# Issuing a kernel's loads in halves at four points of TensorE's progress

## The chip, the cores and the metric

The kernel runs on one core of one Trainium2 chip. The metric is device time in microseconds (us) of one execution; medians are of all runs of a job unless "fast" is said. A run is called slow when it is over 1.5% above the fastest run of its kernel. Ratios below are the mean time of one kernel's fast runs over that of the other's in the same rounds, so they are not quite the ratio of the medians quoted. In the views "PE" is TensorE and "PEld" its weight loads; "DVE", "ACT", "POOL" and "SP" are VectorE, ScalarE, GpSimd and SyncE, and a "q" behind a name is that engine's sequencer.

## The reference, cut to what matters

```python
B, Sq, D = 8, 112, 640
H, Sk, Dh = 32, 512, 192          # all inputs bf16
q = (x @ wq).reshape(B, Sq, H, Dh).transpose(0, 2, 1, 3)
p = softmax(einsum("bhqd,bhkd->bhqk", q, k_cache) * Dh ** -0.5)
o = einsum("bhqk,bhkd->bhqd", p, v_cache)
return o.transpose(0, 2, 1, 3).reshape(B, Sq, H * Dh) @ wo
```

K and V are 50 MB each and are read once, beside 7.9 MB each of wq and wo. So a load stream runs through the whole kernel.

## The kernel before

The work is cut into 64 units: eight head groups of four heads, times eight batches. In unit u TensorE does the scores S of unit u, PV of unit u-1, some tiles of the Q projection (Q) and of the output projection (O), the transposes T of unit u-1's output, and more Q or O tiles. The order is fixed. In the code, W(engine, semaphore, n) makes an engine wait until a semaphore has reached n; NU is the number of units, NK and NV the numbers of K and V buffers. In the views kr is a K buffer, kt its transpose, vs a V buffer, os the normalized output, and L840, L854, L863, L805 and L821 are the lines of S, PV, T, Q and O.

```python
for u in range(NU + 1):                 # TensorE
    if u < NU: do_S(u)                  # 96 matmuls, waits for K transposed by DVE
    if u > 0:  do_PV(u - 1)             # 16 matmuls, waits for V
    for it in items_at[u][0]: do(it)    # Q or O tiles
    if u > 0:  do_T(u - 1)              # waits for DVE's normalization of PV
    for it in items_at[u][1]: do(it)
```

DVE takes K's four transposes for unit u+2, the normalization NM of unit u-1 and the O evacuations strictly in this order. So a K that is late also holds up NM, and with it T on TensorE:

```python
for u in range(NU + 1):                 # DVE
    do_KT(u + 2, 0); do_KT(u + 2, 1)    # the first waits for K of u+2 and for S of u
    if u > 0: do_NM(u - 1)              # sums, 1/x, product into os_, which T reads
    do_KT(u + 2, 2) ...                 # cut: O evacuations, the last transpose
```

SP issues all loads. K and V have four buffers each. K needs a buffer whose transposes are done, V one whose PV is done:

```python
def load_k(u):
    if u >= NK: W(sp, vKT, 4 * (u - NK + 1))
    sp.dma_start(kr[u % NK]..., k_cache[...]).then_inc(mK[u % NK], 16)          # 768 KB
def load_v(u):
    if u >= NV: W(sp, pPV, u - NV + 1)
    for h in range(2):
        sp.dma_start(vs[u % NV][..., h, ...], v_cache[...]).then_inc(mV[u % NV], 16)  # 384 KB
...
for u in range(3, NU):
    load_k(u)
    load_v(u)
    if b == 3 and g + 2 < NG: load_wq(g + 2)    # 960 KB in one DMA
    if b == 6 and g + 1 < NG: load_wo(g + 1)    # 960 KB
```

V's wait is for the PV of four units back. When that ends, SP issues V(u), perhaps weights, and K(u+1) in a row: one burst per unit.

## Time and profile before

Median 472.49 us of 4 runs (468.73 to 478.7). The profiled run took 480.98 us and counts as slow (2.6% above the fastest).

The page of the kernel before; the digits are tenths of busy share, and of the granted TensorE clock, in 40 slices of the span.

```profile
span 479.1 us, 20206 instructions
PE 410.1 (86%) x8920; PEld 298.9 (62%) x8920; DVE 320.2 (67%) x634; ACT 220.9 (46%) x421; POOL 76.8 (16%) x280
PE   5859699999779999886999997779998878999893
PEclk9988899999979999998999999889998998999998
DMA  8997678989549798866689897576986864778711
q1 hardware_dynamic: 90256, 118.70, 74.7%
q8 instruction: 72, 1.18, 1.0%
PE 68%; DMA 10%; issue 10%; DVE 5%; SPq 5%; ACT 1%; DVEq 0%
```

TensorE is the busiest engine and most of the chain that ended last. It is idle for 479.1 - 410.1 = 69 us, the clock dips below full in some slices, and the DMA share swings from 4 to 9 tenths between neighbouring slices. The q8 line is easily passed over: 72 packets of 1.18 MB in all, 16 KB each, of kind "instruction". TensorE has 8920 matmuls and 8920 weight loads; 17840 / 72 = 248, so about one packet for every 250 of its instructions.

The view of waits of the kernel before (engine, line, what it waited for: us in total, times, longest):

```profile
PE ps L854 <- issue: 21.6, 8, 4.8
PE ps L840 <- issue: 14.1, 13, 3.3
PE ps L805 <- issue: 4.0, 3, 2.6
PE ps L863 <- DVE os L964: 7.6, 7, 3.3
DVE kt L952 <- DMA kr<-in_k_cache_dram: 20.5, 8, 4.3
```

"issue" means that the engine stood still and waited for nothing that the profile shows. With two lines of 2.8 us for L863 and L821, TensorE's waits of this kind add up to 45.3 us. L863 is T, which waits for DVE's NM: 7.6 us. What these waits are shows when the records of TensorE's instructions (matmuls, weight loads and those of its sequencer) are counted through in order: in the kernel before, in the changed kernel and in every run below, each "issue" wait of TensorE over 0.2 us after the first 10 us begins at the same place, 192 to 196 instructions past a multiple of 256. Below, the 256 instructions from one such place to the next are called a block, and the instruction packet that follows in order on a block's beginning (the one for the next block) a fetch.

One such wait in the timeline of the kernel before, TensorE's rows only (start, length, what, count, idle before and its releaser):

```profile
214.93 0.33 PE L854 MATMUL ps<-vs,pT 128*128 128x193 bf16 x2 [1.05 <-issue]
218.06 1.36 PE L840 MATMUL ps<-qT,kt 32*128 32x112 bf16 x96
219.35 0.59 PE L854 MATMUL ps<-vs,pT 128*128 128x193 bf16 x5
224.20 1.96 PE L854 MATMUL ps<-vs,pT 128*128 128x193 bf16 x11 [4.25 <-issue]
```

TensorE stops in the middle of PV, after 5 of 16 matmuls, where the program has no semaphore wait at all. The same stretch in 1 us windows (columns: window, its length, busy share of PE, PEld, DVE, ACT and POOL with instruction counts, then clock, DMA share, GB/s):

```profile
214.00:215.00 1.00, 0.07 (x1) 0.07 (x1) 0.35 (x1) 0.47 (x2) 0.00 (x0) 1.00 0.00 0
215.00:216.00 1.00, 1.00 (x7) 0.58 (x7) 0.63 (x4) 0.00 (x0) 0.17 (x1) 1.00 0.00 0
218.00:219.00 1.00, 1.00 (x77) 0.94 (x80) 0.96 (x2) 0.08 (x1) 0.00 (x0) 1.00 1.09 365
221.00:222.00 1.00, 0.00 (x0) 0.00 (x0) 0.16 (x1) 0.30 (x1) 0.00 (x0) 1.00 1.17 415
224.00:225.00 1.00, 0.80 (x6) 0.74 (x7) 0.00 (x0) 0.00 (x0) 0.00 (x0) 0.50 0.23 92
```

The loads go from nothing to 415 GB/s and back, and the clock drops to 0.50 at 223.1 us, while TensorE still stands, and stays there until 230.0. The trace's packet records add the last piece: the instruction packet that comes next in order here started at 221.86 us, 5.5 us into a burst whose packets began at 216.3, and TensorE resumed 1.4 us after it had landed.

### The profile page before, as it was taken

The page shows a single profiled execution, that of the slowest core. Times are in us where ns is not written, and L with a number is a line of the kernel's source. Part 1 is how long each engine was busy: PE and PEld are TensorE (multiplying, and loading weights), DVE is VectorE, ACT ScalarE, POOL GpSimd, SP SyncE. Part 2 cuts the span into 40 slices and gives each one's busy share as a digit, 9 for nine tenths or more (in the row PEclk, how much of TensorE's full clock was granted, in tenths as well). Part 3 has the DMA queues.
Part 4 walks back from the last instruction along what each step waited for, and adds up shares of the span by engine and source line. Part 5 has one row for each costly group of instructions (what it writes and reads, how often), then busy time and mean ns, then how long its engine had stood idle before and what let it go on. Part 6 is the DMA issues. An engine that isn't in the chain of part 4 may idle for free.

```text
span 479.1 us, 20206 instructions
## 1 busy us (share of the span) xinstructions
PE 410.1 (86%) x8920; PEld 298.9 (62%) x8920; DVE 320.2 (67%) x634; ACT 220.9 (46%) x421; POOL 76.8 (16%) x280
## 2 busy tenths in 40 slices
PE   5859699999779999886999997779998878999893
PEld 3436477766647777654777665547776555776672
DVE  2555478777657778755687778456785754788952
ACT  2535255455425555452455554336553553455440
POOL 1300122012110122101221122001230100111110
PEclk9988899999979999998999999889998998999998
DMA  8997678989549798866689897576986864778711
GB/s 311 360 367 247 216 267 264 311 251 341 191 137 332 257 313 289 297 216 218 234 277 299 270 319 233 166 234 217 342 276 206 275 235 148 263 232 297 233 44 34
DMA packets 90348, 120.04 MB, mean 251 GB/s; under 512 B 3472, under 2 KB 82064, under 8 KB 90256
## 3 DMA queue, kind: packets, MB, share of 16 engines
q1 hardware_dynamic: 90256, 118.70, 74.7%
q8 instruction: 72, 1.18, 1.0%
q14 instruction: 20, 0.16, 0.1%
HBM read 117.54 MB, written 1.15 MB: 248 GB/s over the span
## 4 chain that ended last, share of the span: by engine, by line
PE 68%; DMA 10%; issue 10%; DVE 5%; SPq 5%; ACT 1%; DVEq 0%
PE ps L821 17%; PE ps L854 16%; PE ps L840 15%; PE ps L805 14%; DMA kr<-in_k_cache_dram 10%; PE ps L863 5%; SPq L1088 3%; DVE kt L952 2%; DVE os L964 2%; SPq L1067 1%; SPq L1080 0%; PE ps L810 0%; ACT pT L910 0%; DVE rinv L960 0%; ACT oT L919 0%
## 5 line engine op out<-in xcount | busy, mean ns | idle before, releaser
L952 DVE STREAM_TRANSPOSE kt<-kr 128x384 int32<-128x384 int32 x256 | 208.5, 862 | 93.3 <-PE ps L840 72.8
L910 ACT ACTIVATE pT<-ps 128x448 bf16<-128x448 f32 x256 | 118.7, 548 | 92.3 <-PE ps L840 92.3
L854 PE MATMUL ps<-vs,pT 128*128 128x193 bf16 x1024 | 102.8, 254 | 22.7 <-issue 21.6
L821 PE MATMUL ps<-wos,oT 128*128 128x320 bf16 x672 | 113.3, 307 | 3.6 <-issue 2.8
L854 PEld LDWEIGHTS ps<-vs,pT 128*128 128x128 bf16 x1024 | 85.9, 100 | 30.5 <-issue 24.5
L840 PE MATMUL ps<-qT,kt 32*128 32x112 bf16 x6144 | 91.5, 210 | 14.8 <-issue 14.1
L840 PEld LDWEIGHTS ps<-qT,kt 32*128 32x128 bf16 x6144 | 79.0, 94 | 35.3 <-issue 31.7
L805 PE MATMUL ps<-xT,wqs 128*128 128x448 bf16 x420 | 96.2, 366 | 4.0 <-issue 4.0
L902 ACT ACTIVATE qT<-ps 128x448 bf16<-128x448 f32 x96 | 52.2, 545 | 92.1 <-PE ps L805 83.7
L821 PEld LDWEIGHTS ps<-wos,oT 128*128 128x128 bf16 x672 | 64.9, 101 | 34.4 <-issue 6.1
L919 ACT ACTIVATE oT<-ps 128x672 bf16<-128x672 bf16 x64 | 46.8, 731 | 59.3 <-PE ps L863 59.3
L1052 POOL TENSOR_SCALAR bad<-rinv 112x4 f32<-112x4 f32 x64 | 14.6, 228 | 363.6 <-DVE rinv L960 363.6
L964 DVE TENSOR_TENSOR os<-ps,rinv 112x768 bf16<-112x768 f32 x64 | 61.3, 958 | 2.5 <-DVE rinv L960 0.4
L805 PEld LDWEIGHTS ps<-xT,wqs 128*128 128x128 bf16 x420 | 40.8, 101 | 34.9 <-issue 9.8
L978 DVE TENSOR_TENSOR acc<-ps,acc 128x320 f32<-128x320 f32 x84 | 40.3, 480 | 11.3 <-PE ps L821 11.1
L863 PE MATMUL ps<-ident,os 112*128 112x112 bf16 x384 | 31.3, 219 | 10.5 <-DVE os L964 7.6
L863 PEld LDWEIGHTS ps<-ident,os 112*128 112x128 bf16 x384 | 22.1, 100 | 24.5 <-DVE os L964 21.5
L1041 POOL COPY wqs<-wqr 128x384 bf16<-128x384 bf16 x70 | 33.2, 507 | 18.4 <-DMA wqr<-in_wq_dram 16.5
L957 DVE TENSOR_REDUCE sm<-ps 112x4 f32<-112x8 f32 x64 | 10.2, 159 | 30.4 <-PE ps L854 30.3
L810 PE MATMUL ps<-xT,wqs 128*32 128x448 bf16 x240 | 14.9, 404 | 1.2 <-ACT xT L891 0.8
L1053 POOL TENSOR_SCALAR bad<-rinv 112x4 f32<-112x4 f32 x64 | 14.5, 226 | 4.0
L1055 POOL TENSOR_TENSOR cnt<-cnt,bad 112x8 f32<-112x8 f32 x64 | 12.9, 201 | 5.3
(30 smaller groups left out, 50.0 us busy)
## 6 DMA issues: line engine op xcount, KB each, us to landing
kr<-in_k_cache_dram SPq DMA_DIRECT2D x64, 768.0 KB, 7.1
vs<-in_v_cache_dram SPq DMA_DIRECT2D x128, 384.0 KB, 4.4
wos<-in_wo_dram SPq DMA_DIRECT2D x8, 960.0 KB, 8.6
wqr<-in_wq_dram SPq DMA_DIRECT2D x7, 960.0 KB, 8.3
out_dram<-xs SPq DMA_DIRECT2D x7, 160.0 KB, 2.7
wqs<-in_wq_dram SPq DMA_DIRECT2D x1, 960.0 KB, 6.4
xs<-in_x_dram SPq DMA_DIRECT2D x1, 640.0 KB, 4.3
xs<-in_x_dram SPq DMA_DIRECT2D x1, 480.0 KB, 8.5
```

The costliest lines, as they stand in the source:

```text
L805: mm = pe.matmul(ps[:, bank(it), 0:HQ], wqs[:, g % 2, dc, 128 * c:128 * (c + 1)], rhs, start=(dc == 0), stop=(dc == DC - 1))
L821: mm = pe.matmul(ps[:, bank(it), 0:HO], oT[:, c, 128 * m:128 * (m + 1)], wos[:, g % 2, c, HO * h:HO * (h + 1)], start=(c == 0), stop=(c == 5))
L840: mm = pe.matmul(ps[:, a, SQ * t:SQ * (t + 1)], kt[u % 2][p, t, c // 2, :, c % 2], qT[g % 2][p, c, SQ * b:SQ * (b + 1)], start=(c == 0), s ...
L854: mm = pe.matmul(pv[:, k, e, o0:o0 + DH + 1], pT[u % 2][:, a, t, :], vs[u % NV][:, a, t // 2, v0:v0 + DH + 1], start=(t == 0), stop=(t == ...
L863: mm = pe.transpose(psb[:, 4, o0:o0 + SQ], os_[u % 2][:, 128 * j:128 * (j + 1)], ident[0:SQ, 0:SQ])
L902: act.activation(qT[g % 2][:, c, HQ * h:HQ * (h + 1)], ps[:, bank(it), 0:HQ], ACTF.Copy).then_inc(aQ, 1)
L910: act.activation(pT[u % 2][:, a, :, 0:SQ], ps[:, a, 0:4 * SQ].rearrange("p (t q) -> p t q", t=4), ACTF.Exp, scale=scale).then_inc(aEX, 1)
L919: act.activation(oT[:, :, SQ * b:SQ * (b + 1)].rearrange("p (k c) q -> p k c q", k=2), src.rearrange("p k (c q) -> p k c q", c=3), ACTF.Co ...
L952: dve.transpose(dst, src).then_inc(vKT, 1)
L964: dve.tensor_tensor(os_[u % 2][:].rearrange("p (k e d) -> p k e d", k=2, e=2), pv[0:SQ, :, :, 1:1 + DH], rinv[:, u % 4, :].rearrange("p (k ...
L978: ins = dve.tensor_tensor(ob[:, m, cs] if g == NG - 1 else acc[:, m, cs], src, acc[:, m, cs], op=ALU.add)
L1041: ins = gp.tensor_copy(wqs[:, g % 2, dc, :].rearrange("p (k e a i) -> p e k a i", k=3, e=2, a=4)[:, e], wqr[:, dc, :].rearrange("p (a k i ...
```

## The change

The intent is an even load stream. K is halved as V already was; weights are cut into chunks of 160 and 192 KB. SP issues a piece after S, after PV, after the first items and after the second items of every unit, weights after PV. K is loaded three units ahead and V two. No compute instruction moves; outside SP only three wait counts change. The core of the diff (cuts marked):

```diff
-            for u in range(3, NU):
-                load_k(u)
-                load_v(u)
+            for u in range(NU):
+                W(sp, pS, 4 * (u + 1))
+                if u + 3 < NU:
+                    load_k(u + 3, 0)
+                W(sp, pPV, u)
+                if u + 3 < NU:
+                    load_k(u + 3, 1)
                 g, b = divmod(u, B)
-                if b == 3 and g + 2 < NG:
-                    load_wq(g + 2)
-                if b == 6 and g + 1 < NG:
-                    load_wo(g + 1)
+                if b < 3 and g + 2 < NG:
+                    for c in range(2 * b, min(2 * b + 2, DC)):
+                        load_wq(g + 2, c)
+                if b >= 3 and g + 1 < NG:
+                    load_wo(g + 1, b - 3)
+                # cut: the sixth wo chunk, and wo of group 0 in unit 0
+                if items_at[u][0]:
+                    after(items_at[u][0][-1])
+                if u + 2 < NU:
+                    load_v(u + 2, 0)
+                if items_at[u][1]:
+                    after(items_at[u][1][-1])
+                if u + 2 < NU:
+                    load_v(u + 2, 1)
```

At the start, K of unit 1 and V of unit 0 wait for one Q tile each, all of wq for group 1 follows, then K of unit 2 and V of unit 1 (not shown).

More of the change, by code (lines that the diff above doesn't have):

```diff
@@ L817, in do_O @@
                 if m == 0 and h == 0:
-                    W(pe, mWO[g % 2], 16 * (g // 2 + 1))
+                    W(pe, mWO[g % 2], 96 * (g // 2 + 1))
                 bank_free(pe, it)
@@ L947, in do_KT @@
                 if t == 0:
-                    W(dve, mK[u % NK], 16 * (u // NK + 1))
+                    W(dve, mK[u % NK], 32 * (u // NK + 1))
                     W(dve, pS, 4 * (u - 1))
@@ L1036, in reorder @@
                 if dc == 0:
-                    W(gp, mWQ[1], 16 * g)
+                    W(gp, mWQ[1], 16 * DC * g)
                     if g >= 2:
@@ L1063, in load_x, with load_wq0, load_wq, load_wo @@
                     "(m p) d -> p m d", p=128)).then_inc(mX[j], 16)
-            def load_wq(g):
+            def load_wq0():
+                sp.dma_start(wqs[:, 0], wq[:, 0:4 * DH].rearrange("(c p) n -> p c n", p=128)).then_inc(mWQ[0], 16)
+            def load_wq(g, c):
                 W(sp, gW, DC * (g - 1))
-                sp.dma_start(wqs[:, 0] if g == 0 else wqr[:], wq[:, 4 * DH * g:4 * DH * (g + 1)].rearrange(
-                    "(c p) n -> p c n", p=128)).then_inc(mWQ[min(g, 1)], 16)
-            def load_wo(g):
+                sp.dma_start(wqr[:, c, :], wq[128 * c:128 * (c + 1), 4 * DH * g:4 * DH * (g + 1)]).then_inc(mWQ[1], 16)
+            def load_wo(g, c):
                 if g >= 2:
                     W(sp, pO, 2 * MT * (g - 1))
-                sp.dma_start(wos[:, g % 2], wo[4 * DH * g:4 * DH * (g + 1)].rearrange("(c p) d -> p c d", p=128)
-                             ).then_inc(mWO[g % 2], 16)
-            def load_k(u):
+                r = 4 * DH * g + 128 * c
+                sp.dma_start(wos[:, g % 2, c, :], wo[r:r + 128]).then_inc(mWO[g % 2], 16)
+            def load_k(u, h):
                 g, b = divmod(u, B)
@@ L1079, in load_k, with load_v @@
                     W(sp, vKT, 4 * (u - NK + 1))
-                sp.dma_start(kr[u % NK][:].rearrange("p s d -> p (s d)"),
-                             k_cache[b, 4 * g:4 * g + 4].rearrange("a (j s) d -> (a j) (s d)", s=16)).then_inc(mK[u % NK], 16)
-            def load_v(u):
+                sp.dma_start(kr[u % NK][:, 8 * h:8 * h + 8].rearrange("p s d -> p (s d)"),
+                             k_cache[b, 4 * g:4 * g + 4].rearrange("a (j h s) d -> (a j) h (s d)", h=2, s=8)[:, h]
+                             ).then_inc(mK[u % NK], 16)
+            def load_v(u, h):
                 g, b = divmod(u, B)
@@ L1086, in load_v @@
                     W(sp, pPV, u - NV + 1)
-                for h in range(2):
-                    sp.dma_start(vs[u % NV][:, :, h, 32:32 + 2 * DH],
-                                 v_cache[b, 4 * g:4 * g + 4].rearrange("a (m h t) d -> h m a (t d)", h=2, t=2)[h]
-                                 ).then_inc(mV[u % NV], 16)
-            load_x(0)
-            load_wq(0)
-            load_k(0)
-            load_x(1)
-            load_k(1)
-            load_v(0)
-            load_wq(1)
-            load_v(1)
@@ L1100, in _ @@
-            load_k(2)
-            load_wo(0)
-            load_v(2)
-            for u in range(3, NU):
-                load_k(u)
-                load_v(u)
-                g, b = divmod(u, B)
-                if b == 3 and g + 2 < NG:
-                    load_wq(g + 2)
-                if b == 6 and g + 1 < NG:
-                    load_wo(g + 1)
+                sp.dma_start(vs[u % NV][:, :, h, 32:32 + 2 * DH],
+                             v_cache[b, 4 * g:4 * g + 4].rearrange("a (m h t) d -> h m a (t d)", h=2, t=2)[h]
+                             ).then_inc(mV[u % NV], 16)
@@ new lines, in after @@
+            def after(it):
+                if it[0] == "Q":
+                    W(sp, pQ, q_index[it[1:]] + 1)
+                else:
+                    W(sp, pO, o_index[it] + 1)
+            load_x(0)
+            load_wq0()
+            for h in range(2):
+                load_k(0, h)
+            load_x(1)
+            for n, fn, u in ((1, load_k, 1), (3, load_v, 0)):
+                for h in range(2):
+                    after(order[n - 1 + h])
+                    fn(u, h)
+            for c in range(DC):
+                load_wq(1, c)
@@ new lines, in _ @@
+            after(order[5])
+            for h in range(2):
+                load_k(2, h)
+            for h in range(2):
+                load_v(1, h)
+            for u in range(NU):
[5 more added lines that the diff above has]
+                    load_k(u + 3, 1)
+                g, b = divmod(u, B)
+                if b < 3 and g + 2 < NG:
[3 more added lines that the diff above has]
+                    load_wo(g + 1, b - 3)
+                if b == 0 and g >= 1:
+                    load_wo(g, 5)
+                if u == 0:
+                    for c in range(6):
+                        load_wo(0, c)
+                if items_at[u][0]:
[6 more added lines that the diff above has]
+                    load_v(u + 2, 1)
```

## The prediction

> **What bounds the kernel now.** TensorE. In the timeline an undisturbed unit takes 5.71 us from one score stage to the next (231.83 to 237.53), TensorE busy throughout. The shortest spacings of a head group's eight units add up to 47.7 us. Seven groups and the shorter last one would be 372 us; the trace has 442 us between first and last score stage. About 70 us is disturbance: 28 TensorE gaps over 0.7 us (52 us together), and windows at clock 0.5 after them (35 us of busy time at half speed).
>
> **What the gaps are.** Most are put down to "issue", nothing the profile shows (longest 4.8 us; 10% of the chain). They lie every 256 TensorE instructions and end 1.3 to 1.6 us after a 16 KB packet of queue 8 (about 1.0 us each) lands. [...] A fetch on quiet DMA (block begun at 140.33 us) starts 1.3 us later and is usable after 3.9 us; a block lasts 4.5 to 5.5 us, so that fits. A block begun at 214.93 was fetched at 221.86, near the end of a burst of V, wo and K, and TensorE stood 4.25 us. The kernel issues V, K and often 960 KB of weights together once per unit: 4 to 6.5 us of full DMA, then quiet (DMA share 1.0 and 0.0 in 1 us stretches). K landing late (DVE transposes wait 20.5 us in 8 waits) gives a few smaller gaps.
>
> **What the change does.** No compute instruction moves; only SP's list and three wait counts differ. 384 KB pieces go out after S, after PV, after the first items and at the unit's end, 1.3 to 1.7 us apart; each takes about 1.0 us at the bursts' 385 GB/s. Weights follow in chunks of 160 to 192 KB. The queue before a fetch shrinks from up to 6.5 us to 1 to 1.6 us. The long fetch stalls and most half-clock windows should go, leaving 10 us in short ones (estimate: a third of the blocks have only 0.6 to 0.8 us of slack).
>
> **What it costs.** More SP issues (0.5 us each, off the path). Prefetch is shorter: K's second half is issued 4.4 us before DVE needs it; a lone 384 KB piece took 3.3 us at best. DVE has almost no slack before T, so some lateness shows. The mean rate wanted rises to about 305 GB/s.
>
> **Sum.** 17 (first score stage) + 372 + 13 (tail) = 402; + 6 first group still loading much at once, + 10 residual fetch stalls, + 4 half clock and late K: **422 us**, range 402 to 450. Faster by over 2%: 0.93; within: 0.05; slower: 0.02.
>
> **What would show it.** Right: TensorE gaps over 2 us gone; "issue" under 20 us in the waits; spacing near 5.7 us in nearly all units; clock above 0.98; DMA share even at 0.75 to 0.9 over the slices. Wrong: "issue" gaps as long as before (bursts don't delay the fetch), or DVE waiting for K in most units.
>
> **What would make it wrong.** Pieces queue up anyway, since one unit's traffic is 80 to 85% of its time; K's latency above 4.4 us becomes the period; the fetch's delay is set by something other than queued bytes.

The 4.5 to 5.5 us for a block were the author's estimate, and so is the slack behind the 10 us; in the trace of the kernel before, the blocks last 4.7 to 10.1 us from start to start, stalls included, with a median of 6.1.

## The result

Median 445.27 us of 4 runs (442.45 to 449.84) against 472.49 us; ratio of the fast runs 0.9429, 95% interval 0.9336 to 0.9523. The repeat on another chip (e5 below) gave 0.945. The changed kernel is 5.7% faster, where the prediction had 422 us, about 10.6%.

The page of the changed kernel (a fast run), the same lines:

```profile
span 444.3 us, 20578 instructions
PE 399.6 (90%) x8920; PEld 293.0 (66%) x8920; DVE 317.5 (71%) x634; ACT 220.8 (50%) x421; POOL 76.8 (17%) x280
PE   4956999989979999998999899879999999998992
PEclk9998799999998999999999999989999999999998
DMA  7879799998887989998799899878889988999731
q1 hardware_dynamic: 100560, 118.71, 84.3%
q8 instruction: 71, 1.16, 1.1%
PE 68%; DMA 16%; DVE 6%; issue 5%; SPq 2%; POOL 1%; ACT 0%; DVEq 0%; POOLq 0%
```

The DMA slices are even now. TensorE's idle time is 444.3 - 399.6 = 44.7 us, 24.3 less than before, and its busy time is 10.5 us less although it executes the same instructions. That second part is nearly all the clock: nine windows at 0.5 before (35 us of busy time in them), four after (15.5 us), and half of the difference is 9.7 us. 24.3 + 10.5 is the whole 34.8 us between the two profiles. (The medians differ by 27 us, because the profile before was a slow run.)

The waits of the changed kernel:

```profile
PE ps L854 <- issue: 5.0, 4, 2.1
PE ps L840 <- issue: 4.6, 3, 2.8
PE ps L805 <- issue: 0.8, 1, 0.8
PE ps L863 <- DVE os L964: 17.7, 17, 4.6
DVE kt L952 <- DMA kr<-in_k_cache_dram: 38.3, 21, 7.5
```

TensorE's issue waits fell from 45.3 to 10.6 us. But DVE's waits for K nearly doubled, and T's waits for DVE rose from 7.6 to 17.7 us: +10.1 us against -34.7 us, a net of -24.6 us, which matches the idle time. The gain has a price, which one wait of T behind a late K shows in the timeline of the changed kernel (DVE's rows, then TensorE's):

```profile
389.31 1.57 DVE L952 STREAM_TRANSPOSE kt<-kr 128x384 int32<-128x384 int32 x2 [1.44 <-DMA kr<-in_k_cache_dram]
391.22 0.96 DVE L964 TENSOR_TENSOR os<-ps,rinv 112x768 bf16<-112x768 f32 x1
...
390.53 0.98 PE L821 MATMUL ps<-wos,oT 128*128 128x320 bf16 x6
392.23 0.47 PE L863 MATMUL ps<-ident,os 112*128 112x112 bf16 x6 [0.73 <-DVE os L964]
```

K came 1.44 us late for the transposes; the normalization behind them ended late, and TensorE stood 0.73 us before T.

The trace's records allow one more measure. For every block of 256 TensorE instructions, take the time from the block's first instruction to the start of the instruction packet that follows in order (the packet for the next block), leaving out the first eight blocks and the last:

```
kernel                        median us   longest us
before                        3.14        7.53
changed                       2.08        5.66
no K or V traffic (e3)        0.79        3.89
```

Where TensorE waited for a packet, it resumed 1.2 to 1.7 us after that packet had landed, in every one of these kernels. So the stall is set by when the packet starts, and that depends on the load traffic. Single values vary: a repeat of the changed kernel (e5) has 2.21 and 6.28 us.

### The profile page after: what moved, and what is told of

Its sections match the earlier page's. It is cut to its first block, busy times and chain, and to the rows that moved or that the text cites. A ratio compares the mean times of both kernels' runs of the same rounds, so it can differ in the third digit from the quotient of the medians.

```text
span 444.3 us, 20578 instructions
## 1 busy us (share of the span) xinstructions
PE 399.6 (90%) x8920; PEld 293.0 (66%) x8920; DVE 317.5 (71%) x634; ACT 220.8 (50%) x421; POOL 76.8 (17%) x280
## 3 DMA queue, kind: packets, MB, share of 16 engines
q1 hardware_dynamic: 100560, 118.71, 84.3%
## 4 chain that ended last, share of the span: by engine, by line
PE 68%; DMA 16%; DVE 6%; issue 5%; SPq 2%; POOL 1%; ACT 0%; DVEq 0%; POOLq 0%
PE ps L854 17%; PE ps L821 16%; PE ps L840 15%; DMA kr<-in_k_cache_dram 14%; PE ps L805 13%; PE ps L863 5%; DVE os L964 3%; DVE kt L952 3%; PE ps L810 1%; DMA wqr<-in_wq_dram 1%; POOL wqs L1041 1%; DMA xs<-in_x_dram 1%; SPq L1070 1%; SPq L1076 1%; PE ps L785 1%
## 5 line engine op out<-in xcount | busy, mean ns | idle before, releaser
L821 PE MATMUL ps<-wos,oT 128*128 128x320 bf16 x672 | 109.6, 300 | 1.1 <-ACT oT L919 0.8
L854 PE MATMUL ps<-vs,pT 128*128 128x193 bf16 x1024 | 99.4, 249 | 6.1 <-issue 5.0
L840 PEld LDWEIGHTS ps<-qT,kt 32*128 32x128 bf16 x6144 | 78.5, 94 | 24.3 <-issue 20.2
L805 PE MATMUL ps<-xT,wqs 128*128 128x448 bf16 x420 | 93.5, 359 | 0.9 <-issue 0.8
L840 PE MATMUL ps<-qT,kt 32*128 32x112 bf16 x6144 | 89.1, 210 | 5.3 <-issue 4.6
L854 PEld LDWEIGHTS ps<-vs,pT 128*128 128x128 bf16 x1024 | 83.9, 98 | 12.9 <-issue 7.1
L821 PEld LDWEIGHTS ps<-wos,oT 128*128 128x128 bf16 x672 | 63.1, 98 | 29.0 <-issue 1.4
L964 DVE TENSOR_TENSOR os<-ps,rinv 112x768 bf16<-112x768 f32 x64 | 61.3, 958 | 2.5 <-DVE rinv L960 0.4
L863 PE MATMUL ps<-ident,os 112*128 112x112 bf16 x384 | 30.4, 216 | 17.9 <-DVE os L964 17.7
L863 PEld LDWEIGHTS ps<-ident,os 112*128 112x128 bf16 x384 | 21.0, 99 | 34.9 <-DVE os L964 34.0
L1041 POOL COPY wqs<-wqr 128x384 bf16<-128x384 bf16 x70 | 33.2, 507 | 24.3 <-DMA wqr<-in_wq_dram 22.4
L957 DVE TENSOR_REDUCE sm<-ps 112x4 f32<-112x8 f32 x64 | 10.1, 158 | 11.7 <-PE ps L854 11.5
L810 PE MATMUL ps<-xT,wqs 128*32 128x448 bf16 x240 | 15.8, 422 | 1.2 <-ACT xT L891 0.8
L960 DVE RECIPROCAL rinv<-sm 112x4 f32<-112x4 f32 x64 | 11.4, 178 | 3.4
```

The source lines that it names most:

```text
L805: mm = pe.matmul(ps[:, bank(it), 0:HQ], wqs[:, g % 2, dc, 128 * c:128 * (c + 1)], rhs, start=(dc == 0), stop=(dc == DC - 1))
L821: mm = pe.matmul(ps[:, bank(it), 0:HO], oT[:, c, 128 * m:128 * (m + 1)], wos[:, g % 2, c, HO * h:HO * (h + 1)], start=(c == 0), stop=(c == 5))
L840: mm = pe.matmul(ps[:, a, SQ * t:SQ * (t + 1)], kt[u % 2][p, t, c // 2, :, c % 2], qT[g % 2][p, c, SQ * b:SQ * (b + 1)], start=(c == 0), s ...
L854: mm = pe.matmul(pv[:, k, e, o0:o0 + DH + 1], pT[u % 2][:, a, t, :], vs[u % NV][:, a, t // 2, v0:v0 + DH + 1], start=(t == 0), stop=(t == ...
L863: mm = pe.transpose(psb[:, 4, o0:o0 + SQ], os_[u % 2][:, 128 * j:128 * (j + 1)], ident[0:SQ, 0:SQ])
L964: dve.tensor_tensor(os_[u % 2][:].rearrange("p (k e d) -> p k e d", k=2, e=2), pv[0:SQ, :, :, 1:1 + DH], rinv[:, u % 4, :].rearrange("p (k ...
```

## The experiments

Theory: TensorE's instruction packets wait behind queued loads, and the change works by shortening what is queued at one time. Rivals: A, small pieces help as such; B, spreading K and V alone does it, weights don't matter; C, the gaps belong to the fetch however quiet the queues are; D, the kernel before lost its time to late K. Two questions came up with the result: what the late K costs, and what the start costs.

All twelve runs in one table. "Issue" is the sum of TensorE's waits for issue, "T for DVE" that of L863 for L964, "K" that of DVE's transposes for K, all from the view of waits. The kernel before had 45.3, 7.6 and 20.5 there, the changed one 10.6, 17.7 and 38.3.

```
run                           fast median  ratio to before  issue  T for DVE  K     clock
e1_one_point                  473.6        none             26.0   26.3       62.6  0.976
e2_weights_lumped             462.5        none             10.2   33.9       65.7  0.966
e3_no_kv_traffic              421.6        none              6.7    6.1       10.0  0.993
e4_k_one_unit_earlier         443.0        none             12.0   10.8       20.4  0.978
e5_after_again                444.4        0.945            12.3   14.7       36.9  0.982
e6_start                      439.6        0.934            11.5   10.8       24.5  0.983
e7_start_and_k                433.3        0.9199           16.8    1.0        2.2  0.991
e8_before_k_early             476.6        1.0106           48.2    1.0        5.3  0.961
e9_k_start_again              435.8        0.9199           19.7    1.0        2.2  0.986
e10_weights_lumped_k_early    431.3        none             15.4    1.0        2.2  0.982
e11_one_point_k_early         464.4        0.9781           40.6    1.0        2.2  0.965
e12_two_points                435.6        0.9345            7.4   12.8       31.8  0.989
```

e1 to e4 ran on one chip, e5 to e8 on a second, e9 to e12 on a third. Beside e1 to e4 only one run of the kernel before counted as fast (460.56 us), so no ratio was given; those four are compared with each other, and with the changed kernel only across chips (445.3 us in its first job, 444.4 in e5). The fast medians of the kernel before were 471.6 us beside e5 to e8 and 473.0 us beside e9 to e12. All profiles in this table are of fast runs. e10 and e12 had only two fast runs each; their medians over all runs were 434.7 and 441.1 us. Beside e5 to e8 only 5 of 11 runs of the kernel before were fast; the interval of e11, 0.9709 to 0.9854, reaches over 0.98.

### e1: the same pieces, one point of issue

```diff
                 W(sp, pS, 4 * (u + 1))
+                W(sp, pPV, u)
                 if u + 3 < NU:
                     load_k(u + 3, 0)
-                W(sp, pPV, u)
-                if items_at[u][0]:
-                    after(items_at[u][0][-1])
-                if items_at[u][1]:
-                    after(items_at[u][1][-1])
```

> The changed kernel, with the same pieces and chunks and the same units ahead, but all of a unit's pieces issued at one point, after PV. If the gain is that an instruction fetch no longer stands behind a burst (my theory): most of the gain goes, 460 to 480 us, with TensorE issue gaps over 2 us and half-clock windows back as in the kernel before. If the gain is from smaller pieces and chunks as such, whenever they are issued (rival A): it stays at 440 to 450 us.

473.6 us, in the range expected, where e4 on the same chip took 443.0 and the changed kernel on others 444 to 445. Halves and chunks issued in one go bring nothing, so rival A falls. The loss has two parts, issue waits of 26.0 us and late K of 62.6 us; e11 takes them apart.

### e2: weights in two lumps per group

```diff
-                if b < 3 and g + 2 < NG:
-                    for c in range(2 * b, min(2 * b + 2, DC)):
+                if b == 3 and g + 2 < NG:
+                    for c in range(DC):
                         load_wq(g + 2, c)
-                if b >= 3 and g + 1 < NG:
-                    load_wo(g + 1, b - 3)
-                if b == 0 and g >= 1:
-                    load_wo(g, 5)
+                if b == 6 and g + 1 < NG:
+                    for c in range(6):
+                        load_wo(g + 1, c)
```

> The changed kernel with the weights not spread: all five wq chunks in unit 3 of a group, all six wo chunks in unit 6, as the kernel before had them. Theory: only those two units of each group get a burst (0.96 MB, 2.5 us more), so some of the fetch gaps and late K come back: 10 to 15 us slower than the changed kernel, 455 to 460. If the spread of K and V alone carries the gain (rival B): 440 to 448. In the first group it also takes the second wq load out of the start, which may give back up to 6 us.

462.5 us, slower than expected, and by late K alone, where I had expected fetch gaps to return as well. The issue waits did not grow (10.2 us). T's waits for DVE did, to 33.9 us, and DVE's for K to 65.7 us: the lump stands in front of the next K.

### e3: no K and V traffic (wrong result)

K and V are loaded for the first four units only and then used again; the instruction streams stay as they are.

```diff
-                    W(dve, mK[u % NK], 32 * (u // NK + 1))
+                    W(dve, mK[u % NK], 32)
-                W(pe, mV[u % NV], 32 * (u // NV + 1))
+                W(pe, mV[u % NV], 32)
                 if u >= NK:        # and the same for V
-                    W(sp, vKT, 4 * (u - NK + 1))
+                    return
```

> The changed kernel without K and V loads after the first four units (the result is wrong on purpose; compute, instruction streams and weights stay). Theory: with quiet DMA queues nothing delays a fetch and K is never late; spacing 5.7 us in all units, issue gaps under 5 us in sum after the start, clock 0.99; 402 to 415 us. If the gaps at every 256 instructions come from the fetch itself, however quiet the queues (rival C): they stay, 430 us or more.

421.6 us, with a relative error of 1.27 as intended. The page:

```profile
span 423.0 us, 20220 instructions
PE   4965889999999999999999999989999999999992
PEclk9998999999999999999999999999999999999998
DMA  7789101210112111121112111021011010100021
```

After the first sixth TensorE is at 9 tenths nearly throughout, and the median unit follows the one before in 5.71 us. Issue waits are 6.7 us in all, about half of them in the start, where the traffic still is. Rival C falls: the same instructions fetched over quiet queues hardly ever stall. It also gives a floor for this TensorE program with this start, about 420 us. I had expected 402 to 415, with the same errors in the sum as in the prediction (see below).

### e4, e6, e7: K earlier, and another start

e4 loads K one unit further ahead from unit 7 on. The buffers allow it, because K(u) is transposed two units before its own scores.

```diff
-                if u + 3 < NU:
-                    load_k(u + 3, 0)      # and the second half alike
+                ks = [w for w in ([u + 3] if u < 7 else [10, 11] if u == 7 else [u + 4]) if w < NU]
+                for w in ks:
+                    load_k(w, 0)
```

e6 changes the start alone: K of units 1 and 2 and V of unit 0 go out at once, wq of group 1 after them, and the second wq load and the first wo load are spread over later units.

```diff
-            for n, fn, u in ((1, load_k, 1), (3, load_v, 0)):
+            for u in (1, 2):
                 for h in range(2):
-                    after(order[n - 1 + h])
-                    fn(u, h)
+                    load_k(u, h)
+            for h in range(2):
+                load_v(0, h)
+            after(order[2])
             for c in range(DC):
                 load_wq(1, c)
             after(order[5])
             for h in range(2):
-                load_k(2, h)
+                load_k(3, h)
 # cut: in group 0, wq of group 2 in units 2 to 4; wo of group 0 in units 0 and 1
```

e7 has that start and K four units ahead from the first unit on. e5 is the changed kernel again, beside them.

> The changed kernel, K loads one unit further ahead from unit 7 on (slots allow it, no new buffer). Theory: the late K of the changed kernel (transposes waiting 38 us in 21 waits, and the TensorE gaps of 0.7 to 1.4 us before the transposes of the output) go after the first group; the fetch gaps stay: 8 to 12 us faster than the changed kernel, 433 to 438. If K's lateness was hidden behind fetch stalls: within 3 us of it.

> The changed kernel once more, as the measure of the three beside it: 443 to 447 us.

> The changed kernel with its start alone rearranged: K and V of the first units issued in the order of need without waiting for Q tiles, the second wq load and the first wo load spread over units 0 to 4 so that SP does not stand behind GpSimd's reordering. Theory: the first group's excess (13 us over its 47.7, of which TensorE gaps of 4.65 and 3.98 us waiting for late K) is the start's queueing and SP's order: 6 to 10 us faster than the changed kernel. Rival: the first group is limited by the bytes it needs, whatever their order: within 3 us. The fuller queue may bring a fetch gap or two in the first 30 us.

> The rearranged start and K one unit further ahead from the first unit on. Theory: late K and the start's gaps both gone, what is left over the run without traffic (422 us) is residual fetch gaps and half clock, about 10 us: 430 to 436 us, faster than both kernels. Transposes wait for K under 10 us in all.

e4 took 443.0 us, less of a gain than expected and within 3 us of the changed kernel (on other chips), which is what the rival, lateness hidden behind fetch stalls, forecast. T's waits for DVE did fall, to 10.8 us, most of it the two waits of 4.5 and 3.4 us in the first group, which e4 leaves alone. e4 alone does not decide between the two; e6 and e7, side by side on one chip, show what the earlier K is worth once the start is mended, 439.6 - 433.3 = 6.3 us. e6 took 439.6 us, 4.8 less than e5 beside it and short of the 6 to 10 expected (over all six runs, two of them slow, 441.6 and so 2.9 less, which is no more than the rival's 3 us): the first group shortened, but a few fetch stalls came with its fuller queue (the longest in the first 50 us is 2.55 us). e7 took 433.3 us, 11.1 us less than e5, and its waits confirm both repairs, though its issue waits are higher than e5's (16.8 against 12.3 us):

```profile
PE ps L863 <- DVE os L964: 1.0, 2, 0.7
DVE kt L952 <- DMA kr<-in_k_cache_dram: 2.2, 1, 2.2
```

e7 is correct and faster than both kernels, by 8% against the kernel before (ratio 0.9199, interval 0.9139 to 0.926), and e9 repeated it on another chip with the same ratio.

### e8: the kernel before with K earlier

Bursts and whole pieces stay; each K is issued ahead of the previous unit's V.

```diff
+            load_k(3)
             load_v(2)
             for u in range(3, NU):
-                load_k(u)
+                if u + 1 < NU:
+                    load_k(u + 1)
                 load_v(u)
```

> The kernel before, unsplit and in bursts, with each K issued ahead of the previous unit's V, so one unit earlier. If the kernel before lost its time to fetches behind bursts (theory): late K (20 us of transposes' waits) goes, the issue gaps and half-clock windows stay, 462 to 474 us. If its gaps were late K at bottom (rival D): 440 to 455 us.

```profile
PE ps L854 <- issue: 20.0, 8, 4.2
PE ps L840 <- issue: 17.5, 14, 3.9
PE ps L863 <- DVE os L964: 1.0, 2, 0.7
DVE kt L952 <- DMA kr<-in_k_cache_dram: 5.3, 2, 3.2
```

476.6 us, above the 462 to 474 expected and no faster than the kernel before (ratio 1.0106, interval 1.002 to 1.0192; why it was a little slower is not known). Late K is gone, and the issue waits are all there (48.2 us in sum, in a fast run). Rival D falls: the kernel before lost its time to the fetch, and mending its few late K alone gained nothing.

### e9, e10, e11: which part of the change acts through what

e9 is e7 again. e10 is e7 with e2's lumps of weights, e11 is e7 with e1's single point of issue (edits as shown there).

> The kernel with rearranged start and K one unit earlier once more (433 us before), as the measure of the two made from it: 430 to 437 us.

> That kernel with the weights in two lumps per group, as in e2_weights_lumped. There the issue gaps had not grown (8 us after the first 50 us) but transposes waited 66 us for K. If lumps hurt through late K (theory): with K a unit earlier they cost little, within 5 us of the kernel beside it. If they hurt through fetch delay: 8 to 15 us slower.

> That kernel with all of a unit's pieces at one point after PV, as in e1_one_point, which lost by both fetch gaps (26 us) and late K (63 us of waits). With K a unit earlier only the fetch gaps are left. Theory: 450 to 462 us, issue gaps of 20 us or more and half-clock windows back, transposes' waits for K under 15 us. If the one point hurt through late K alone: within 5 us of the kernel beside it.

e10: 434.7 us over all runs against 435.8 for e9. With K early enough, spreading the weights is worth nothing measurable. In the changed kernel it mattered (e2) only because K's lead was short. So rival B is right about the fetch, and wrong about the changed kernel as it stands.

e11: 464.4 us, 28.6 us more than e9, with K's waits at 2.2 us in both. The first two lines are e9's, the other three e11's:

```profile
PE ps L840 <- issue: 8.4, 7, 3.4
PE ps L854 <- issue: 6.2, 6, 1.8
PE ps L854 <- issue: 17.9, 7, 4.6
PE ps L840 <- issue: 11.3, 9, 3.1
DVE kt L952 <- DMA kr<-in_k_cache_dram: 2.2, 1, 2.2
```

The same pieces, the same lead in units, the same weights; only the points of issue differ, and issue waits go from 19.7 to 40.6 us and the clock from 0.986 to 0.965. By the block measure the median delay of a packet goes from 2.30 to 3.04 us. TensorE's busy time at half clock goes from 6.8 to 24.2 us, which costs half of the difference, 8.7 us; with the 20.9 us of issue waits that is 29.6 of the 33.2 us between the two profiles. The points of issue carry the gain, through the fetch. (It went a little above the expected 462.)

### e12: two points in place of four

```diff
                 if u + 3 < NU:
                     load_k(u + 3, 0)
-                W(sp, pPV, u)
                 if u + 3 < NU:
                     load_k(u + 3, 1)
+                W(sp, pPV, u)
 ...
-                if items_at[u][1]:
-                    after(items_at[u][1][-1])
```

> The changed kernel with two points in place of four: both K pieces after S, both V pieces after the first items, weights after PV as they are. A fetch may stand behind 0.77 MB (2 us) in place of 0.38 MB (1 us), but K's second piece goes out 1.45 us earlier. Theory: a little more fetch delay, a little less late K: 440 to 450 us, near the changed kernel's 444; so halving would be worth little beside moving the issue points.

441.1 us over all five runs, within the expected range, and 435.6 us in the two fast ones, below it; issue waits 7.4 us. Two points for K and V show as no worse than four (the changed kernel did not run beside it). Spacing the halves of K and of V apart is not what the gain rests on.

## Why the prediction was right, and where its sizes were off

- **The bound and the gaps.** Right. TensorE bounds the kernel (busy for 86% of the span, 68% of the chain that ended last), and the waits for "issue" go with its instruction packets: 16 KB each, one for about 250 instructions, stalls at one place of every 256, and TensorE back 1.2 to 1.7 us after a packet's landing. They cost 45.3 us before, 48.2 in e8, and 6.7 with quiet queues.
- **What the change removes.** Right in kind and nearly in size. Issue waits were to be under 20 us and are 10.6; the even DMA slices came; the clock was to be above 0.98 and is 0.976 (0.982 in e5). "TensorE gaps over 2 us gone" is not quite so: after the start two are left (2.1 and 2.84 us). "Spacing near 5.7 us in nearly all units" did not come: 33 of the 63 spacings are under 6.0 us, 31 before, and even e3 has 43, so this sign was badly chosen; what shrank are the long ones (a tenth are over 7.5 us, 9.9 before).
- **"K's second half is issued 4.4 us before DVE needs it ... some lateness shows, a few us in all."** The mechanism was right and the size too small. T's waits for DVE rose by 10.1 us; e7 takes them away. The sign of a wrong prediction, DVE waiting for K in most units, did not come: 21 waits in 64 units.
- **The sum.** The gain was about half of the forecast one, 27 us for 50, and 445.3 us lies near the upper end of the stated range of 402 to 450: the direction rests on the mechanism, but the wide range held with only 5 us to spare. 422 predicted, 444.3 in the profile. Four terms make up the difference. The first score stage began at 18.4 us, not 17. The tail from the last score stage to the end of the span is 19.2 us; I wrote 13, because I counted to the last matmul and forgot what follows it, though the profile before already showed 19.2. The first group exceeded its 47.7 us by 13 us, not 6. The other seven groups exceeded theirs by 21.7 us, not 14. That is 1.4 + 6.2 + 7 + 7.7 = 22.3 us. So about a third of the miss is an arithmetic slip at the tail, a third the start, and a third late K and residual fetch stalls. e3's 421.6 us, without traffic, leaves no room for 422 with the loads of K and V on top and this start and tail.
- **"The queue before a fetch shrinks ... to 1 to 1.6 us."** Too hopeful. The median delay fell from 3.14 to 2.08 us, but single fetches still started 5.66 us after their block. Bursts are not all that delays a fetch.

What stays open: why a packet of the instruction queue has to wait so long behind loads. The fetch of 221.86 us started only 5.5 us into the burst; where it waited until then, no run here tells. Nor does a queue of loads in motion explain the whole delay. That block began at 214.93 us and the burst's first packet at 216.3, 1.39 us later, while over quiet queues a fetch starts after 0.79 us (median of e3); SP had issued the first load at 215.28. And in e3 the blocks begun between 117 and 123 and between 267 and 273 us still waited 2.5 to 3.9 us, with a mean DMA share of 0.2 to 0.4 meanwhile. Nor is it settled why the remaining stalls fall at about the same places of the program (near 120 to 133, 205 to 217 and 282 to 295 us in several runs).

## What to carry to other kernels

When TensorE waits for "issue" in the middle of a stage, look at the instruction queue of the profile and count instructions between the gaps. Here TensorE's 17840 matmuls and weight loads went with 72 instruction packets, whose median start was 3.14 us after their block began with the loads in bursts and 0.79 us without K and V traffic. Tie loads to the progress of the busiest engine so that they go out evenly (5.7% here), but then check that every load still has enough lead, because pacing shortened the lead (T's waits for DVE rose from 7.6 to 17.7 us). Take leads from where free buffers allow it (e7, with its mended start, was 11.1 us faster than e5) before cutting pieces smaller (nothing by itself in e1).

## What else the traces show

- What the fetches cost: with a load stream of 251 GB/s (the mean of the page) TensorE's waits for "issue" took 45.3 us of 479. On quiet queues a block was usable about 3.9 us after the one before was begun (an estimate from the kernel before: begun at 140.33 us, packet landed at 142.83, and 1.2 to 1.7 us to resume), while the middle half of e3's blocks lasted 5.1 to 5.6 us.
- What smaller K pieces cost: the data queue's share went from 74.7% of 479.1 us to 84.3% of 444.3 us for the same bytes, 4.6% more engine time; K's packets alone, of 3072 in place of 6144 bytes, went from 129.6 to 149.7 us of all 16 engines. The smaller pieces bought nothing by themselves (e1), and in e12 the two halves went out together without loss. No run had whole K pieces at the new points.
- How long a fetch waited to start: a median of 3.14 us before and 3.04 us in e11 (longest 7.5 and 7.1 us), against 0.79 us without traffic (longest 3.89).
- What came before the clock's drops to 0.50: in the two kernels there are 13 before the last matmul, ten of them 3.41 us long and three 6.83 us. They began during a TensorE wait or up to 1.5 us after one: ten with waits for "issue" of 2.10 to 4.75 us, three with waits of T for DVE (3.28, 3.98 and 4.65 us). Length alone does not decide: after a gap of 2.61 us in the kernel before (297.32 to 299.93 us) the clock stayed. In the 3.41 us before each of the 13 drops TensorE had been busy for at most 1.52 us; but in the 3.41 us before 299.93 us it had been busy for only 0.80, so that does not decide either. The windows of the changed kernel around one drop, columns as before:

```profile
131.00:132.00 1.00, 0.00 (x0) 0.00 (x0) 1.00 (x2) 1.00 (x3) 0.00 (x0) 1.00 0.97 311
132.00:133.00 1.00, 0.00 (x0) 0.00 (x0) 0.49 (x1) 0.63 (x2) 0.00 (x0) 0.92 1.11 326
134.00:135.00 1.00, 1.00 (x9) 0.93 (x7) 0.00 (x0) 0.00 (x0) 0.00 (x0) 0.50 0.47 183
137.00:138.00 1.00, 1.00 (x13) 0.81 (x12) 1.00 (x3) 0.53 (x1) 0.00 (x0) 1.00 0.64 243
```

By the trace's clock records the clock is at 0.50 from 132.8 to 136.3 us, with a stall of 2.10 us (130.94 to 133.04) before it.
